# Ten token tiles of an output projection as 64-row products, and a dense stage whose order waits are PE's own

## The chip, the cores and the metric

The kernel runs on one core of one Trainium2 chip. The metric is the device time of one execution in microseconds: 1581.37 us for the kernel before, the median of 3 runs from 1580.71 to 1581.43.

PE is the engine of matrix products, with PEld its weight loads; ACT and DVE are the two engines that read the products' banks (PSUM), POOL a third vector engine without them, and SP issues most DMAs. Each engine takes its own instructions in the order in which the program lists them and waits on semaphores for the others.

## The reference, cut to what matters

```python
x = A_x                                   # 2048 tokens x 512
xn = layernorm(x)
qkv = xn @ wqkv                           # 32 heads of 16
p = softmax(q @ k.T * 16 ** -0.5)         # per head, 2048 x 2048
s = (p @ v) @ wo                          # 512 x 512
g = silu(gelu(xn @ w1 + b1) @ w2 + b2)    # hidden 1376
out = x + s * g
```

All inputs and the output are float32.

## The kernel before

*Number format.* A float32 product is made of three products of a reduced float32 form: each operand is split into a high and a low part, and `mm3` (L77) multiplies high by high, high by low and low by high into one bank. Scores take the three parts as 48 rows of one product instead; the products of probabilities and values (L804) are plain float32.

*Halves of PE.* A product with at most 64 contraction rows uses half of the array's rows. The kernel places such products in two kinds by rows: row half `a` = 0 stands on partitions 0 to 63, `a` = 1 on 64 to 127, and two products in different halves can run side by side. [...]

*Dense stage* (up to about 475 us). Layernorm and transposes come first. Then `run` (L614) issues lists of 64-row products for both halves in turn: the value projection (`quad`, L702), the query, key and hidden projections (`half`, L692) and the second matrix of the feed-forward part (`down`, L645). Between them `fill` (L563) places score products of the first heads' maxima (`s_one`, L203, whose product stands at L183), which DVE reduces (L189). All dense products go through `mm` (L583). It keeps for each bank (`key`) which half wrote it last and as which product. When a bank changes halves and that product isn't known to have ended (`prog["seen"]`, raised by `taken`, L577, since an older score product must have been reduced before a newer one takes its bank), `mm` needs a token: `mark` (L600) puts a copy of one element on ACT (L604) or DVE (L602), which waits for the newest product, and the next product of the new half waits for that copy. `down` sets marks ahead of need (`mark_early`, L608, at its fourth pair; two marks on DVE in its last but one part), `quad` one at its seventh pair.

*Attention stage.* It has 512 steps, `n`, in the loop at L966: 32 units `u` (4 heads and 512 queries each) by 16 blocks of 128 keys. A step's order on PE is written out as a string (`ORDER`, L40). T is a transposed score tile of 128 keys by 512 queries (`t_one`, L732, product L739), whose exponential ACT writes to SBUF (L741). S, X and Y are score products for maxima of later units (L183). V is the four value products of the step before (`pv_step`, L798), on the full rows in four column groups. Up to step 491 a step is `TSXTTSTYV`; from 492 on, when no maxima are left, `TTTTV`. The first two T of a step stand on half 1, the other two on half 0. T takes four banks in turn; a T waits until ACT has read its bank.

*Output stage inside the loop.* `todo` holds further work by step and place: what `at(n, f, ..., pos)` registers is issued after the T with that number (0 to 3) of step `n`. The output projection has 16 token tiles of 128. The first ten (`NW`) are placed from step `DONE` = 492 on, one each two steps:

- `load_gx` (L852), four steps before: two DMAs on SP bring the gate's input and x into `gx`, which has four buffers
- `w_token` (L881), two steps before: ACT copies the tile's four 128 x 128 blocks of the attention output to the high part (L876), POOL subtracts for the low part (L877)
- `w_mul` (L892): `mm3` for two of the four blocks at the tile's first step and for two at the second, after the step's last T, as products of all 128 rows; they add to one bank of a ring of three (`s_tile`, L92)
- `gate` (L863), at the first step: a tanh on ACT (L865) and a multiplication on DVE (L866)
- `w_out` (L913), at the second step: `w_gate` on DVE (L905) reads the bank, `w_add` on POOL (L910) adds x, and SP stores (L911)

Gates and loads of the last six tiles are placed at odd steps in between; their products come after the loop (L985 on), with moves and division of the last unit's output (`o_move`, `o_den`, `o_div`).

## Time and profile before

| What | Value |
|---|---|
| median of 3 runs | 1581.37 us |
| the profiled execution, its own time | 1580.84 us |
| its span | 1579.0 us |
| granted PE clock, mean of the core | 1.00 |
| PE busy | 1572.2 us in 12144 products |
| DVE busy | 1396.2 us in 2292 instructions |
| ACT busy | 1247.6 us in 2489 instructions |
| POOL busy | 373.6 us in 394 instructions |
| full-row products at L80 in the late stage | 10 tiles of 12, from 1492.7 us |

An instruction row of the timeline gives start, duration, engine, source line, operation, what it writes and reads, and in brackets the idle time of the engine before it with what ended it. Equal instructions in a row are joined (x2 and so on): the duration is then from the first start to the last end. A product's end is modelled, so starts tell more than durations. Rows of products name the output's tile: `pst` and `ps` are banks of different pools, `pv` that of the value products.

### The profile page before, as it was taken

What the parts mean: (1) busy time and instruction counts of PE and PEld (TensorE: products, weight loads), DVE (VectorE), ACT (ScalarE), POOL (GpSimd) and SP (SyncE); (2) the same over time, 40 slices, a digit from 0 to 9 for tenths busy, and PEclk for the clock granted to TensorE, in tenths of its full rate; (3) what the DMA queues carried; (4) which work ended last, traced back from release to release, by engine and by line L of the source; (5) the groups of instructions that cost most, each with busy time, mean ns of one, the idle gap of its engine ahead of it and who ended that gap; (6) DMA issues with size and microseconds to landing.
All of it is one profiled execution on the core that took longest, in us unless ns stands there. A gap on an engine that the chain in (4) does not pass through costs nothing.

```text
span 1579.0 us, 31736 instructions
## 1 busy us (share of the span) xinstructions
PE 1572.2 (100%) x12144; PEld 949.2 (60%) x12144; DVE 1396.2 (88%) x2292; ACT 1247.6 (79%) x2489; POOL 373.6 (24%) x394
## 2 busy tenths in 40 slices
PE   9999999999999999999999999999999999999998
PEld 8899899999994444444444444444444444444445
DVE  7599898989988999999999999999999999999734
ACT  4333443434339999999999999999999999999984
POOL 4145575766641001001000100100100000000143
PEclk9999999999999999999999999999999999999999
DMA  6626343454322114111511511421150111110252
GB/s 207 151 59 154 116 138 99 147 150 122 123 84 76 43 33 68 29 36 42 82 30 29 69 38 34 56 45 29 30 76 24 33 29 36 36 30 22 60 194 101
DMA packets 74647, 116.86 MB, mean 74 GB/s; under 512 B 23012, under 2 KB 24292, under 8 KB 73320
## 3 DMA queue, kind: packets, MB, share of 16 engines
q1 hardware_dynamic: 70748, 101.89, 24.1%
q0 software_dynamic: 3264, 12.35, 4.7%
q8 instruction: 96, 1.57, 0.5%
q10 hardware_dynamic: 484, 0.60, 0.1%
q14 instruction: 55, 0.45, 0.1%
HBM read 84.35 MB, written 25.97 MB: 70 GB/s over the span
## 4 chain that ended last, share of the span: by engine, by line
PE 98%; DVE 1%; DMA 0%; issue 0%; ACT 0%; DVEq 0%
PE pv L804 33%; PE pst L739 21%; PE ps L590 13%; PE ps L183 10%; PE pst L590 7%; PE ps L739 7%; PE ps L80 3%; PE pv L590 2%; PE ps L458 1%; PE pst L80 1%; DVE st L417 0%; PE pst L440 0%; DMA xt<-in_x 0%; PE pst L458 0%; DVE slot L75 0%; DVE xn L431 0%
## 5 line engine op out<-in xcount | busy, mean ns | idle before, releaser
L189 DVE TENSOR_REDUCE mx<-ps 128x2 f32<-128x512 f32 x2048 | 1298.3, 685 | 118.6 <-PE ps L183 33.0
L741 ACT ACTIVATE slot<-pst 128x512 f32<-128x512 f32 x1533 | 825.9, 603 | 19.9 <-PE pst L739 10.5
L804 PE MATMUL pv<-slot,vsb 128*32 128x512 f32 x4096 | 545.3, 605 | 0.0
L183 PE MATMUL ps<-kt,slot 48*128 48x512 f32 x1364 | 376.4, 366 | 0.0
L739 PE MATMUL pst<-qt,kt 50*128 50x512 f32 x1149 | 372.3, 431 | 0.6 <-DVE gt L672 0.4
L739 PEld LDWEIGHTS pst<-qt,kt 50*128 50x128 f32 x1149 | 188.6, 184 | 288.3 <-ACT slot L741 261.8
L741 ACT ACTIVATE slot<-ps 128x512 f32<-128x512 f32 x515 | 311.2, 605 | 2.7 <-PE ps L183 1.8
L183 PEld LDWEIGHTS ps<-kt,slot 48*128 48x128 f32 x1364 | 224.7, 184 | 8.2 <-DVE mx L189 5.9
L590 PE MATMUL ps<-slot,w1h 64*128 64x512 f32 x1088 | 218.0, 393 | 0.0
L183 PE MATMUL ps<-kt,qz 48*128 48x512 f32 x512 | 212.8, 416 | 0.0
L183 PE MATMUL ps<-slot,slot 48*128 48x512 f32 x598 | 165.5, 366 | 0.0
L739 PE MATMUL ps<-qt,kt 50*128 50x512 f32 x387 | 159.7, 415 | 0.0
L590 PEld LDWEIGHTS ps<-slot,w1h 64*128 64x128 f32 x1088 | 151.2, 185 | 8.2 <-ACT junk L604 2.4
L590 PE MATMUL ps<-slot,w1l 64*128 64x512 f32 x544 | 141.8, 393 | 0.0
L804 PEld LDWEIGHTS pv<-slot,vsb 128*32 128x32 f32 x4096 | 80.6, 108 | 100.0 <-issue 91.8
L377 POOL TENSOR_TENSOR hl<-hg,hh 128x512 fp32r<-128x512 f32 x76 | 96.7, 1295 | 129.6 <-ACT hh L376 97.5
L250 POOL CAST nmh<-nm 128x16 fp32r<-128x16 f32 x32 | 6.3, 196 | 480.4 <-DVE nm L247 458.0
L604 ACT ACTIVATE junk<-ident_r 1x1 f32<-1x1 f32 x92 | 18.0, 196 | 119.3 <-PE pst L590 116.1
L739 PE MATMUL pst<-qt,slot 50*128 50x512 f32 x384 | 111.2, 414 | 0.0
L183 PEld LDWEIGHTS ps<-kt,qz 48*128 48x128 f32 x512 | 93.7, 183 | 15.6
L183 PEld LDWEIGHTS ps<-slot,slot 48*128 48x128 f32 x598 | 98.3, 184 | 3.1 <-DVE mx L189 2.1
L739 PEld LDWEIGHTS ps<-qt,kt 50*128 50x128 f32 x387 | 71.1, 184 | 42.1 <-ACT slot L741 36.4
(159 smaller groups left out, 1707.2 us busy)
## 6 DMA issues: line engine op xcount, KB each, us to landing
raw<-in_w SPq DMA_DIRECT2D x88, 256.0 KB
qk_h<-hh SPq DMA_DIRECT2D x32, 256.0 KB
qk_l<-hl SPq DMA_DIRECT2D x32, 256.0 KB
qt<-qk_h SPq DMA_DIRECT2D x128, 64.0 KB
slot<-qk_h SPq DMA_DIRECT2D x92, 64.0 KB
g_d<-gt POOLq DMA_DIRECT2D x16, 256.0 KB, 3.8
qt<-qk_l SPq DMA_DIRECT2D x64, 64.0 KB
dn<-den_d SPq DMA_DIRECT2D x32, 128.0 KB
```

Source lines behind the costliest of these rows:

```text
L80: nc.tensor.matmul(ps, lhs[a], rhs[b], start=first and n == 0, stop=last and n == 2)
L183: return nc.tensor.matmul(ps[:, c0:c0 + w], QS[u][r, p, qi * P:(qi + 1) * P], kts[u // NCH % KB][p][r, k0:k0 + w], start=True, stop=True).ins
L189: nc.vector.tensor_reduce(MX[u][:, 2 * p:2 * p + 2, qi, ki][:, heads, parts], ps.rearrange("p (n c) -> p n c", c=HC), axis=AX.X, op=OP.max)
L250: nc.gpsimd.tensor_copy(hl[:, 0], nm)
L377: nc.gpsimd.tensor_sub(hl, raw, hh.bitcast(F32))
L458: nc.tensor.matmul(pq["q", g, c], W1[g][i][:, k * P:(k + 1) * P], (xh, xl)[j][c][:, k], start=n == 0 and k == 0, stop=n == 2 and k == KT - 1)
L590: i = nc.tensor.matmul(ps, lhs[r], rhs[r], start=first, stop=last).ins
L604: i = nc.scalar.activation(junk[:, :1], ident_r[:1, :1].bitcast(F32), AF.Copy).ins
L739: nc.tensor.matmul(ps, kts[g % KB][p][r, k * P:(k + 1) * P], QT[u][r, p, :], start=True, stop=True)
L741: nc.scalar.activation(PT[u, k][:, 2 * p + a, :], ps, AF.Exp, scale=SCALE)
L804: nc.tensor.matmul(PV[u][32 * j:32 * j + 32, :], vsb[:, k, h:h + 32], PT[u, k][:, j, :], start=(k == 0), stop=(k == NT - 1))
```

## The change

Three things change.

1. The first ten token tiles are taken in pairs. `w_two` splits two blocks of both tiles at a time. `w_halves` makes the products of one block of both tiles with 64 rows each: tile `t` on one row half and tile `t + 1` on the other, and at the next step the halves are exchanged. A pair takes four steps; six half products come after the step's second T (`pos=1`) and six after its last. The first product of a step after the pair's first waits for the last one of the step before (`HALF`).
2. Loads and gates are placed by pair: the load three steps before the pair's first step and two before (tile `t + 1`), gates at the first and the second step, both tiles' `w_out` at the fourth.
3. `mark`, `mark_early` and the copies of one element are gone. `mm` waits on PE's own semaphore for the product that wrote the bank last.

```diff
@@ mm
-        token = None
         if not first and writer[key][0] != a and writer[key][1] > prog["seen"]:
-            if not tokens or tokens[-1][0] < writer[key][1]:
-                mark()
-            prog["seen"], token = next(x for x in tokens if x[0] >= writer[key][1])
+            hold = nc.tensor.nop().ins
+            tc.add_manual_dep(hold, writer[key][2], SYNC, reason="other row tile")
+            prog["seen"] = writer[key][1]
         i = nc.tensor.matmul(ps, lhs[r], rhs[r], start=first, stop=last).ins
-        if token is not None:
-            tc.add_manual_dep(i, token, SYNC, reason="other row tile")
...
-        writer[key] = (a, prog["pe"])
+        writer[key] = (a, prog["pe"], i.name)
...
@@ down
-        n = prog["pe"]
-        if (c, f, part) == parts[-2]:
-            run(ops, {2: [lambda: mark(True)], 5: [lambda: mark(True)]})
-        else:
-            run(ops, {3: [lambda: mark_early(n)]})
+        run(ops)
@@ quad
-            hooks = {6: [mark]} if i in (1, 2) else {}
+            hooks = {}
@@ output stage
+    def w_two(t, k0):
+        oh, ol = [wb.tile([P, KT, P], F32R, name=x, bufs=3) for x in ("oh", "ol")]
+        c, i = divmod(t, NCH)
+        src = ot[c][:, k0:k0 + 2, i * P:(i + 2) * P]
+        hi, lo = [w.rearrange("p (k t) s -> p k (t s)", t=2) for w in (oh, ol)]
+        nc.scalar.activation(hi, src, AF.Copy)
+        nc.gpsimd.tensor_sub(lo, src, hi.bitcast(F32))
+        for k in range(2):
+            for j in range(2):
+                OTS[t + j, k0 + k] = (oh[:, 2 * k + j], ol[:, 2 * k + j])
+
+    HALF = {}
+
+    def w_halves(t, k, side):
+        ts = (t, t + 1)
+        if k == 0 and side == 0:
+            for i in ts:
+                PW[i] = [s_tile()[0]]
+        elif k % 2 == 0:
+            hold = nc.tensor.nop().ins
+            tc.add_manual_dep(hold, HALF[0].name, SYNC, reason="row tile done")
+        for n, (x, y) in enumerate(((0, 0), (0, 1), (1, 0))):
+            for a in range(2):
+                i = ts[a ^ side]
+                r = slice(64 * a, 64 * a + 64)
+                HALF[0] = nc.tensor.matmul(PW[i][0], OTS[i, k][x][r], (wo_h, wo_l)[y][r, k],
+                                           start=k == 0 and side == 0 and n == 0,
+                                           stop=k == KT - 1 and side == 1 and n == 2).ins
@@ placement
     for t in range(NW):
-        n = DONE + 2 * t
-        at(n - 4, load_gx, t)
-        at(n - 2, w_token, t)
-        at(n, w_mul, t, KS[:2])
-        at(n, gate, t)
-        at(n + 1, w_mul, t, KS[2:])
-        at(n + 1, w_out, t, nc.gpsimd)
+        n = DONE + 4 * (t // 2)
+        at(n - 3 + t % 2, load_gx, t)
+        if t % 2 == 0:
+            for i in range(4):
+                if i % 2 == 0:
+                    at(n + i - 2, w_two, t, i)
+                for j in range(2):
+                    at(n + i, w_halves, t, i // 2 * 2 + j, i % 2, pos=1 + 2 * j)
+        at(n + t % 2, gate, t)
+        at(n + 3, w_out, t, nc.gpsimd)
```

In the built program 92 copies on ACT, two on DVE and the waits for them are gone; the holds become waits of the next product on PE's own semaphore. PE has 120 products more (120 of full rows become 240 of half rows). ACT and POOL have as many splits as before, and SP as many DMAs.

More of the change, by code (lines that the diff above doesn't have):

```diff
@@ L584, in mm @@
         r = slice(64 * a, 64 * a + 64)
-        token = None
         if not first and writer[key][0] != a and writer[key][1] > prog["seen"]:
-            if not tokens or tokens[-1][0] < writer[key][1]:
-                mark()
-            prog["seen"], token = next(x for x in tokens if x[0] >= writer[key][1])
+            hold = nc.tensor.nop().ins
+            tc.add_manual_dep(hold, writer[key][2], SYNC, reason="other row tile")
+            prog["seen"] = writer[key][1]
         i = nc.tensor.matmul(ps, lhs[r], rhs[r], start=first, stop=last).ins
-        if token is not None:
-            tc.add_manual_dep(i, token, SYNC, reason="other row tile")
         prog["pe"] += 1
         row[a] += 1
-        latest[0] = (prog["pe"], i.name)
-        writer[key] = (a, prog["pe"])
-    tokens, latest = [], [None]
-    def mark(dve=False):
-        if dve:
-            i = nc.vector.tensor_copy(junk[:, 1:], ident_r[:1, :1].bitcast(F32)).ins
-        else:
-            i = nc.scalar.activation(junk[:, :1], ident_r[:1, :1].bitcast(F32), AF.Copy).ins
-        tc.add_manual_dep(i, latest[0][1], SYNC, reason="row tile done")
-        tokens.append((latest[0][0], i.name))
-    def mark_early(n):
-        if prog["seen"] < n:
-            mark()
-    junk = keep_r.tile([1, 2], F32, name="junk")
+        writer[key] = (a, prog["pe"], i.name)
     def run(ops, hooks={}):
@@ L657, in down @@
                                    f == 0 and part == 0 and n == 0, f == FT - 1 and part == 1 and n == 2))
-        n = prog["pe"]
-        if (c, f, part) == parts[-2]:
-            run(ops, {2: [lambda: mark(True)], 5: [lambda: mark(True)]})
-        else:
-            run(ops, {3: [lambda: mark_early(n)]})
+        run(ops)
         if part == 0:
```

## The prediction

> **What bounds the kernel now.** I read the first page, then the busy time by stretch, the chain in order of time, and the timeline of single steps.

> ```profile
> span 1579.0 us, 31736 instructions
> PE 98%; DVE 1%; DMA 0%; issue 0%; ACT 0%; DVEq 0%
> ```

> The profiled run took 1580.84 us: its span and 1.8 us around it, 0.53 under the median 1581.37. The chain is nearly all PE, but a busy PE is a modelled one, so the spacing of starts has to be read instead, stage by stage.

> ```profile
> 600.00:800.00 200.00, 200.00 (x1556) 93.97 (x1555) 188.11 (x312) 197.57 (x389) 24.47 (x37) 1.00 0.26 50
> 1497.50:1556.00 58.50, 58.50 (x326) 27.13 (x324) 20.77 (x26) 49.56 (x98) 27.96 (x20) 1.00 0.48 163
> ```

> Columns: span, then busy PE, PEld, DVE, ACT, POOL, clock, DMA share, GB/s. In the long attention stage, of which the first row is a part, ACT is busy 197.57 of 200, and no edit touches it. In the late stage, where the edited products stand, DVE has little left and ACT is busy 49.56 of 58.50.

> ```profile
> 1497.75 0.99 PE pv L804 x8
> ...
> 1556.20 1.85 PE pv L804 x16
> ```

> These rows of the chain are the value products of steps 494 and 512. 18 steps lie between: 58.45 / 18 = 3.247 us a step, ACT 49.56 / 18 = 2.75 of it. So PE's order sets the late step. One of them:

> ```profile
> 1505.19 0.73 PE L739 MATMUL pst<-qt,kt 50*128 50x512 f32 x3
> 1505.53 0.39 PE L739 MATMUL ps<-qt,kt 50*128 50x512 f32 x1
> 1505.85 0.50 PE L80 MATMUL ps<-wo_h,oh 128*128 128x512 f32 x1
> 1506.18 0.39 PE L80 MATMUL ps<-wo_l,oh 128*128 128x512 f32 x1
> 1506.41 0.39 PE L80 MATMUL ps<-wo_h,ol 128*128 128x512 f32 x1
> ...
> 1507.11 0.39 PE L80 MATMUL ps<-wo_h,ol 128*128 128x512 f32 x1
> 1507.42 1.06 PE L804 MATMUL pv<-slot,vsb 128*32 128x512 f32 x8
> 1508.42 0.51 PE L739 MATMUL pst<-qt,kt 50*128 50x512 f32 x2
> ```

> Four transposed tiles T0 to T3 (L739), six full-array output products (L80), four value products (L804). From the first T to V: 2.23 us; V to the next T: 1.00. A full-array product costs 0.23 (1506.18 to 1506.41). Around them is the loss: 0.32 from the last T to the first product (1505.53 to 1505.85) and 0.33 from that to the second, 0.65 for what two turns of 0.23 would be: 0.19 goes at the change from half arrays to the full array.

> **The change, part by part.**

> *Output products as halves.* Per token 12 products of 128 rows become 24 of 64 rows; two of them, on the two row halves, take the place of one. By step: T0, T1 on the upper half (both stand on rows 64 up), six half products, T2, T3 on the lower half, six half products, V. Each half gets 2 T and 6 products, eight turns, and nothing changes between half and full array before V. What a turn costs is seen in the dense stage, whose products are 64-row pairs already:

> ```profile
> 195.50 0.54 PE L590 MATMUL pst<-w2h,hl 64*128 64x512 f32 x2
> 195.65 0.20 ACT L604 ACTIVATE junk<-ident_r 1x1 f32<-1x1 f32 x1 [1.12 <-PE pst L590]
> 195.91 0.50 PE L590 MATMUL ps<-slot,w1h 64*128 64x512 f32 x1
> 196.25 0.40 PE L590 MATMUL ps<-slot,w1h 64*128 64x512 f32 x2
> 196.48 0.40 PE L183 MATMUL ps<-kt,qz 48*128 48x512 f32 x1
> 196.72 0.39 PE L590 MATMUL ps<-slot,w1l 64*128 64x512 f32 x2
> 196.95 0.63 PE L590 MATMUL ps<-slot,w1h 64*128 64x512 f32 x4
> ```

> Pairs start 0.233 apart (196.25 to 196.95 is three turns), and the first after an empty array takes 0.34 (195.91 to 196.25). The turn from the last product to V is taken as today, 0.31 (1507.11 to 1507.42). So T to V becomes 0.34 + 6 x 0.233 + 0.31 = 2.05 for eight turns, against 2.23: 0.18 a step. That needs the two halves to run as queues of their own, for in the program's order T1 stands before any work of the lower half. The trace shows it: T0, T1 come first and share their rows, yet

> ```profile
> 1505.19 0.50 PE L739 MATMUL pst<-qt,kt 50*128 50x512 f32 x2
> ```

> (a window cut short) has two T starting at once, and the fourth T, the one row named ps, starts 0.34 later, at 1505.53. Taken strictly in order it would be the third turn, 0.57 later. So T2 passed T1. The new order asks for no more: one product waiting on each half. Bounds: 1.94, if the weight load behind the first pair's 0.34 were hidden too, and 2.28, nine turns in strict order (0.34 + 7 x 0.233 + 0.31). I take 2.05, as the row speaks for the pass. [...]

> Nineteen steps give 19 x 0.18 = 3.4 us. The first late step is of another kind:

> ```profile
> 1491.18 1.04 PE L739 MATMUL pst<-qt,kt 50*128 50x512 f32 x3
> 1492.22 0.50 PE L739 MATMUL ps<-qt,kt 50*128 50x512 f32 x1
> 1492.65 0.50 PE L80 MATMUL ps<-wo_h,oh 128*128 128x512 f32 x1
> ...
> 1494.26 1.07 PE L804 MATMUL pv<-slot,vsb 128*32 128x512 f32 x8
> ```

> Here the T wait for ACT to empty their banks, T3 until 1492.22, and all six products wait behind it: 3.08 us to V. In the new order T3's turn comes at 0.34 + 3 x 0.233 = 1.04, just when its bank is free, with products before it. Saved 3.08 - 2.05 = 1.03; between 0.2 (ACT's wait is only moved) and 1.0 I take 1.0.

> *Tail.* POOL now adds token 8 and token 9 after the last step, in front of the split of token 11.

> ```profile
> 1556.13 1.92 PE L804 MATMUL pv<-slot,vsb 128*32 128x512 f32 x16
> 1556.24 0.69 DVE L905 SCALAR_TENSOR_TENSOR gx<-ps,gx 128x512 f32<-128x512 f32 x1 [1.70 <-PE ps L80]
> 1557.01 1.28 POOL L910 TENSOR_TENSOR gx<-gx 128x512 f32<-128x512 f32 x1 [1.33 <-DVE gx L905]
> 1558.24 1.28 POOL L877 TENSOR_TENSOR ol<-ot,oh 128x512 fp32r<-128x512 f32 x1
> 1558.99 1.16 SPq L827 DMA_DIRECT2D ot<-os  x2
> 1561.34 0.39 PE L80 MATMUL pst<-wo_h,ol 128*128 128x512 f32 x1
> 1561.41 0.33 SPq L833 DMA_DIRECT2D den_d<-dr  x1
> ```

> The split (L877) ended at 1559.52; with one more 1.28 it ends at 1560.8, and PE first needs it at 1561.34. SP's moves of the last unit (1558.99) stand behind a store that waits for the second addition; they start about 1.0 later and end at 1561.1, before the store of 1561.41. Between 0 and 0.5 late; I take 0.2.

> *Waits added in the late steps.* In 15 of the 20 steps the first half product waits on PE's own semaphore, for the last product of the step before, seven or eight matmuls back, with the whole V between: nothing. Behind it on PE stands the rest of the step. The split of the tokens into high and low parts (one ACT copy and one POOL subtraction for four 128 x 128 blocks, as many as before) is made two steps ahead, as before: nothing. Two tokens now end together, so the second bank is free one gate (0.69) later; of the three banks only the pair at step 496 takes both of the pair just ended, and its second product comes 0.57 after T0, 1.57 after V's start, against two gates (L905) that end 0.11 + 2 x 0.69 = 1.49 after it: nothing, or 0.2 once.

> *Gates early, loads.* ACT keeps its count, 2.75 a step within 3.07. The row loads stand three steps before their gate in SP's queue, behind two output stores instead of one.

> ```profile
> SPq L911 <- POOL gx L910: 34.9, 9, 6.1
> ```

> SP already stands 34.9 us in the late stage waiting for POOL before a store, and the loads behind it are in time. A second addition on POOL (1.28) makes them that much later, out of a lead of three steps of 3.05, 9 us. Were that cover gone, the gate's tanh would hold the exponentials behind it on ACT by the same amount. I take nothing.

> *Dense waits.* 92 small ACT operations and two on DVE go, each of which let PE wait for ACT to have seen a matmul end. In the new program 12 waits on PE's own semaphore remain, for matmuls at least 11 back (1.3 us at half a turn, 0.117, each), long ended.

> ```profile
> L604 ACT ACTIVATE junk<-ident_r x92: 182/202/205, 56.5 to 473.3; 1x1 f32<-1x1 f32 x92
> ...
>   PEld ps L590: 2.4, 9
> ```

> PE waited for them nine times, 2.4 us of weight loading in all. The fence of the dense stage shows one: the second of the two products at 195.50 starts at 195.65 (0.54 less its own 0.39 later), PE's next at 195.91, 0.26 on where 0.117 is half a turn, and the turn after that is 0.34 instead of 0.23; so the halves lose about 0.2. Bounds are 0 and 2.4; of the nine I count five as large as this one, 1.0. The 92 operations of 0.2 on ACT are no gain by themselves: PE, not ACT, has no gap there.

> Sum: -3.4 - 1.0 - 1.0 + 0.2 = -5.2. From 1580.84 that is 1575.6; at the median, 1576.2.

> **The rivals.**

> *Strict order* (nine turns): 19 x 0.05 longer, the first step 0.8 shorter, dense and tail as above: 0.95 - 0.8 - 1.0 + 0.2 = -0.65, 1580.7. Against it stands the pair at 1505.19; for it, that row shows a pass of one product once a step, while here one is needed at six turns in a row. [...]

> *Cover gone on ACT or SP*: late loads or a backlog before the exponentials. It would show as T waiting for ACT in steps with two extra ACT operations. ACT has 3.07 - 2.75 = 0.32 a step; half of the late gain lost makes -5.2 + 2.2 = -3.0: 1578.4.

> *Slower: each change of hands between T and products empties the half.* If the halves go in order and the weight load of the next product shows at each such change (T1 to product, product to T2, T3 to product), three turns cost 0.34 instead of 0.233 on top of nine: 2.28 + 3 x 0.107 = 2.60 from T to V. That is 19 x 0.37 = 7.0 longer, the first step 0.5 shorter, dense and tail as above: +5.7, 1587.1. It decides from the point where T to V is over 2.23. For it: a wait on a semaphore stands at two of the three places. Against it: in the dense stage the rows at 196.25 to 196.95 change between score and dense products (L183, L590) at the plain 0.233.

> **How the numbers follow.** Forecast 0.60, cover gone 0.14, strict order 0.14, slower 0.12. What a measurement can tell from no change is about 0.2%, 3.2 us. The forecast's own range is 1574 to 1578; strict order and half of the cover-gone case lie within 0.2%, and so does a tenth of the forecast: faster 0.54 + 0.07, rounded to 0.62; slower 0.12 and a little for what I did not see, 0.14; same 0.24. The range goes down to 1573.5 (late steps at 1.95 and dense waits at their bound) and up to 1584.5, past the strict order and into a mild case of the slower one; it leaves out about 0.1 above and 0.05 below.

> **What would show it.** In the new profile: L904 half products in pairs 0.23 apart, T to V 2.05 and the step near 3.05 in the chain; two T no longer starting together but each beside a product. Step 492 near 2.1 to V. No gap of 0.26 to 0.34 at the five dense places. The split of token 11 ending before its first use. Wrong would be: T to V of 2.28 or more; rows of ACT waiting for a load or of T for ACT in the late stage; PE waiting for POOL or a gate; a change in the long attention stage.

## The result and the profile after

| | before | after |
|---|---|---|
| median of 9 runs each, us | 1581.37 (1580.65 to 1581.85) | 1576.81 (1576.40 to 1577.34) |
| profiled execution, its span, us | 1580.84, 1579.0 | 1576.64, 1574.9 |
| first T after the dense stage | 474.00 | 473.26 |
| start of the last value products | 1556.13 | 1551.65 |
| from there to the end | 22.88 | 23.21 |

The ratio of the times is 0.9973 (95% interval 0.9963 to 0.9982): 0.27% faster. The medians differ by 4.56 us, the two profiled executions by 4.20 and their spans by 4.1; the account below goes by the spans. The forecast was a median of 1576.2.

Stretches of the changed kernel, with the columns as before (span, busy PE, PEld, DVE, ACT, POOL, clock, DMA share, GB/s):

```profile
600.00:800.00 200.00, 200.00 (x1555) 94.28 (x1555) 188.06 (x312) 197.61 (x388) 24.48 (x37) 1.00 0.26 50
1493.60:1551.60 58.00, 57.76 (x453) 30.77 (x449) 22.11 (x27) 51.62 (x102) 26.95 (x20) 1.00 0.51 170
```

The attention stage is what it was, with ACT busy 197.61 of 200. The late stage needs less time for a step (3.07 us instead of 3.25), and ACT's busy time in it rose from 49.56 of 58.50 us to 51.62 of 58.00: ACT is still idle at times, and the step still follows PE's turns.

One normal late step of the changed kernel, PE's timeline (start, us, engine, line, operation, tiles):

```profile
1531.20 0.50 PE L715 MATMUL pst<-qt,kt 50*128 50x512 f32 x1
1531.20 0.49 PE L904 MATMUL ps<-wo_h,oh 64*128 64x512 f32 x1
1531.54 0.39 PE L715 MATMUL pst<-qt,kt 50*128 50x512 f32 x1
1531.54 0.39 PE L904 MATMUL ps<-wo_l,oh 64*128 64x512 f32 x1
1531.76 0.39 PE L904 MATMUL ps<-wo_h,oh 64*128 64x512 f32 x1
1531.77 0.39 PE L904 MATMUL ps<-wo_h,ol 64*128 64x512 f32 x1
1532.00 0.39 PE L904 MATMUL ps<-wo_l,oh 64*128 64x512 f32 x1
1532.01 0.40 PE L715 MATMUL pst<-qt,kt 50*128 50x512 f32 x1
1532.23 0.39 PE L904 MATMUL ps<-wo_h,ol 64*128 64x512 f32 x1
1532.24 0.39 PE L715 MATMUL ps<-qt,kt 50*128 50x512 f32 x1
1532.46 0.41 PE L904 MATMUL ps<-wo_h,oh 64*128 64x512 f32 x2
...
1533.27 1.06 PE L780 MATMUL pv<-slot,vsb 128*32 128x512 f32 x8
```

Read it in pairs: a turn is one product on each half, and there are eight, 0.34 after the first and about 0.23 after each other one. T0 (L715) runs beside the first lower product, T1 beside the second. In the program T1 stands ahead of both lower products; it starts 0.34 after the first of them. From T0 to V it is 1533.27 - 1531.20 = 2.07 us.

Where the 4.1 us of span came from, by the starts of V in both traces (steps numbered as in the loop; the two V that the prediction called steps 494 and 512 are those of 493 and 511, and its count of 18 steps between them stands):

| Part | before | after | change |
|---|---|---|---|
| to the first T | 474.00 | 473.26 | -0.74 |
| from there to V of step 491 | 1016.19 | 1016.26 | +0.07 |
| step 492, V to V | 4.07 | 3.16 | -0.91 |
| 17 normal late steps, each | 3.25 | 3.07 | -3.1 |
| steps 496 and 497 together | 6.49 | 6.68 | +0.19 |
| last V to the end | 22.88 | 23.21 | +0.33 |

The changes add up to -4.2 (4.1 by the spans; the rest is rounding). Steps 496 and 497 are the place where the late stage fell short: they should have lost 0.36, as two normal steps do.

### The profile page after: what moved, and what is told of

The parts are those of the page before. It is cut to its first block, busy times and chain, and to the rows that moved or that the text cites. A ratio compares the mean times of both kernels' runs of the same rounds, so it can differ in the third digit from the quotient of the medians.

```text
span 1574.9 us, 31849 instructions
## 1 busy us (share of the span) xinstructions
PE 1567.4 (100%) x12264; PEld 951.9 (60%) x12264; DVE 1396.5 (89%) x2290; ACT 1233.8 (78%) x2397; POOL 371.7 (24%) x394
## 4 chain that ended last, share of the span: by engine, by line
PE 98%; DVE 1%; ACT 0%; DMA 0%; issue 0%; DVEq 0%
PE pv L780 33%; PE pst L715 21%; PE ps L589 12%; PE ps L183 10%; PE pst L589 7%; PE ps L715 7%; PE pv L589 2%; PE ps L904 1%; PE ps L80 1%; PE ps L458 1%; PE pst L80 1%; DVE st L417 0%; DMA xt<-in_x 0%; PE pst L440 0%; PE pst L458 0%
## 5 line engine op out<-in xcount | busy, mean ns | idle before, releaser
L715 PE MATMUL pst<-qt,kt 50*128 50x512 f32 x1149 | 380.1, 429 | 0.6 <-DVE gt L648 0.4
L183 PE MATMUL ps<-kt,slot 48*128 48x512 f32 x1364 | 376.0, 366 | 0.0
L715 PEld LDWEIGHTS pst<-qt,kt 50*128 50x128 f32 x1149 | 192.1, 184 | 288.1 <-ACT slot L717 272.3
L183 PEld LDWEIGHTS ps<-kt,slot 48*128 48x128 f32 x1364 | 224.9, 184 | 8.2 <-DVE mx L189 5.9
L183 PE MATMUL ps<-kt,qz 48*128 48x512 f32 x512 | 213.9, 418 | 0.0
L183 PE MATMUL ps<-slot,slot 48*128 48x512 f32 x598 | 165.3, 366 | 0.0
L715 PE MATMUL ps<-qt,kt 50*128 50x512 f32 x387 | 159.3, 414 | 0.0
L589 PEld LDWEIGHTS ps<-slot,w1h 64*128 64x128 f32 x1088 | 154.5, 185 | 4.5
L370 ACT ACTIVATE hg<-ps,b_sb 128x512 f32<-128x512 f32 x44 | 27.8, 684 | 132.0 <-PE ps L589 120.5
L715 PE MATMUL pst<-qt,slot 50*128 50x512 f32 x384 | 111.3, 414 | 0.0
L183 PEld LDWEIGHTS ps<-kt,qz 48*128 48x128 f32 x512 | 93.7, 183 | 19.4
L183 PEld LDWEIGHTS ps<-slot,slot 48*128 48x128 f32 x598 | 98.4, 184 | 3.3 <-DVE mx L189 2.1
L715 PEld LDWEIGHTS ps<-qt,kt 50*128 50x128 f32 x387 | 71.1, 184 | 42.3 <-ACT slot L717 36.1
```

The costliest lines, as they stand in the source:

```text
L183: return nc.tensor.matmul(ps[:, c0:c0 + w], QS[u][r, p, qi * P:(qi + 1) * P], kts[u // NCH % KB][p][r, k0:k0 + w], start=True, stop=True).ins
L370: nc.scalar.activation(raw, ph.pop(u), AF.Gelu_apprx_tanh, bias=b1_sb[:, u[2]:u[2] + 1])
L589: i = nc.tensor.matmul(ps, lhs[r], rhs[r], start=first, stop=last).ins
L715: nc.tensor.matmul(ps, kts[g % KB][p][r, k * P:(k + 1) * P], QT[u][r, p, :], start=True, stop=True)
```

## The experiments

All start from the changed kernel, except one that edits the kernel before; all but the mended kernel are single edits. Each ran once, except the mended kernel and the changed kernel beside it, so most readings are of one profile; a normal step's T to V differs by at most 0.03 us within a profile. Steps are read from V to V, "T to V" from the first T.

*By halves: how deep a row half's queue is at least.*

```diff
-        for n, (x, y) in enumerate(((0, 0), (0, 1), (1, 0))):
-            for a in range(2):
+        for a in range(2):
+            for n, (x, y) in enumerate(((0, 0), (0, 1), (1, 0))):
                 i = ts[a ^ side]
```

> Only the order inside a group of six half products changes: three on the lower row half, then three on the upper, where the changed kernel alternates. The theory (each row half is a queue of its own in which one product can wait, and PE takes its instructions in program order until the next finds that place full): counted turn by turn, nine turns from the first T to V instead of eight, 2.30 us where the changed kernel has 2.07; 19 steps, +4.4 us, a span near 1579.3. Rival, strict order (no product starts before one that stands ahead of it): twelve turns, 3.00 us, +18 us. Rival, two or more may wait on each half: eight turns, 2.07 us, no change.

The span is 1575.0 us, and T to V in the normal steps 2.07: no change. The theory's count was wrong, and the rival of two or more waiting products right; strict order would have cost 18 us by the count recorded above. (Step 497 is longer here than in the changed kernel; the last experiment takes that up.) The next run measures the depth.

*Deep: six products of one half ahead of anything for the other.* The order inside a late step becomes T0, T1 and six products on the upper half, then T2, T3 and six on the lower.

```diff
+        a = 1 - k % 2
...
-        for n, (x, y) in enumerate(((0, 0), (0, 1), (1, 0))):
-            for a in range(2):
-                i = ts[a ^ side]
+        i = ts[a ^ side]
+        for kk in (k - k % 2, k - k % 2 + 1):
+            for n, (x, y) in enumerate(((0, 0), (0, 1), (1, 0))):
```

> How many products can wait on one row half. In each late step the program's order is T0, T1 and six half products, all on the upper half, then T2, T3 and six half products on the lower. Counted turn by turn, the lower half stands idle until PE has put the upper half's products aside: with two places to wait a step has 13 turns, 3.21 us from T to V; with three 2.98; four 2.75; five 2.51; six 2.28; seven or more eight turns, 2.07 as in the changed kernel. Theory (the queues are no deeper than the two that the order by halves needs): 3.21 us, +1.14 a step, a span near 1597. Rival (deep queues): 2.07 to 2.3, a span of 1575 to 1580.

One step of this kernel, PE's timeline:

```profile
1531.17 0.72 PE L715 MATMUL pst<-qt,kt 50*128 50x512 f32 x2
1531.73 0.40 PE L906 MATMUL ps<-wo_h,oh 64*128 64x512 f32 x1
1531.97 0.39 PE L906 MATMUL ps<-wo_l,oh 64*128 64x512 f32 x1
1532.21 0.39 PE L906 MATMUL ps<-wo_h,ol 64*128 64x512 f32 x1
1532.21 0.50 PE L715 MATMUL pst<-qt,kt 50*128 50x512 f32 x1
...
1534.28 1.06 PE L780 MATMUL pv<-slot,vsb 128*32 128x512 f32 x8
```

Eight products of the upper half stand ahead of T2 in the program. T2 (the row of L715 at 1532.21) starts together with the fifth of them, ahead of the other three. That is the case of three places: 2.98 us was expected, and 0.107 more for T2's turn of 0.34 on a half that stood idle (T3 starts at 1532.55) makes 3.09; measured 3.11, a span of 1594.0. Depth two, the theory, is out by this row: T2 would have started with the sixth. That there are places, and three of them, is the author's count from these rows; the run doesn't tell whether they belong to each half or are shared by both: counted with three shared places, the order by halves has eight turns as well.

*After T: form or place.* All products behind the fourth T.

```diff
-                    at(n + i, w_halves, t, i // 2 * 2 + j, i % 2, pos=1 + 2 * j)
+                    at(n + i, w_halves, t, i // 2 * 2 + j, i % 2, pos=3)
```

> All twelve half products of a step stand behind the fourth T; none stand between the T. The theory (the gain of a normal late step comes from the form of the products, halves instead of the full array, and not from where they stand): eight turns again, T to V 2.05 to 2.10 us in the normal steps. The first late step, whose fourth T waits for its bank at 1.04 us with all products behind it, becomes 2.75 us instead of 2.17, so the span is some 0.6 us over 1574.9. Rival (the place between the T makes the gain): T to V stays at 2.23 or more in every step, a span of 1578 or more.

T to V in the normal steps is 2.06: the place earns nothing there, the form does. Step 492 of this kernel on PE's timeline:

```profile
1490.79 1.06 PE L715 MATMUL pst<-qt,kt 50*128 50x512 f32 x3
1491.84 0.50 PE L715 MATMUL ps<-qt,kt 50*128 50x512 f32 x1
1491.85 0.72 PE L904 MATMUL ps<-wo_h,oh 64*128 64x512 f32 x2
...
1493.67 1.07 PE L780 MATMUL pv<-slot,vsb 128*32 128x512 f32 x8
```

T3 waits until 1491.84 for its bank, and no product starts before it: 2.88 us to V against 2.17 with the products in between (2.75 was expected). So the place is worth 0.71 us, once. The span is 1575.9.

*Full products in between: the price of changing between half rows and the full array.*

```diff
-        for n, (x, y) in enumerate(((0, 0), (0, 1), (1, 0))):
-            for a in range(2):
-                i = ts[a ^ side]
...
+        i = ts[side]
+        mm3(PW[i][0], OTS[i, k], (wo_h[:, k], wo_l[:, k]), k == 0, k == KT - 1)
```

> The products keep their places between the T, but each pair of half products is one full-array product, three per group. The theory (each change between half rows and the full array costs): T0 to T1 0.34, to the first product 0.32, 0.33 and 0.23 within the three, 0.31 to T2, and the same again to V: 3.06 us from T to V instead of 2.07, steps of 4.06, 20 x 1.0 = 20 us more, a span near 1595. Without a cost of the change (ten turns of 0.233, the first 0.34, 0.31 to V) it would be 2.51 us and +9. Rival (the place alone earns): 2.07, no change.

PE's timeline of this kernel, the first half of a step:

```profile
1531.83 0.73 PE L715 MATMUL pst<-qt,kt 50*128 50x512 f32 x2
1532.49 0.50 PE L80 MATMUL ps<-wo_h,oh 128*128 128x512 f32 x1
1532.83 0.39 PE L80 MATMUL ps<-wo_l,oh 128*128 128x512 f32 x1
1533.06 0.39 PE L80 MATMUL ps<-wo_h,ol 128*128 128x512 f32 x1
1533.38 0.50 PE L715 MATMUL pst<-qt,kt 50*128 50x512 f32 x1
```

Each change shows twice, 0.32 before the first product of the new kind (1533.06 to 1533.38) and 0.34 after it (1532.49 to 1532.83), where a turn within a kind is 0.23. T to V is 3.10 (3.06 expected), the span 1594.8 (1595 expected). In this place the same multiplications as full products cost 20 us more than as halves.

*Near wait: when a wait on PE's own semaphore costs.*

```diff
-        elif k % 2 == 0:
+        else:
             hold = nc.tensor.nop().ins
             tc.add_manual_dep(hold, HALF[0].name, SYNC, reason="row tile done")
```

> A wait on PE's own semaphore is added in each of the 20 late steps, ahead of the second group of half products, for the last product of the first group, three products back with two T between (the waits of the changed kernel are for products seven or eight back). The theory (an own wait is free only where the awaited product has long ended): the second group starts when that product has ended, about 0.4 us after its start, which is some 0.2 us later than its turn, and its first turn is 0.34 instead of 0.23: T to V 2.37 us instead of 2.07, 20 x 0.3 = +6 us, a span near 1581. Rival (such a wait costs nothing at any distance): 2.07 and no change.

PE's timeline around one of the added waits:

```profile
1532.61 0.39 PE L904 MATMUL ps<-wo_h,ol 64*128 64x512 f32 x1
1532.61 0.40 PE L715 MATMUL ps<-qt,kt 50*128 50x512 f32 x1
1533.05 0.50 PE L904 MATMUL ps<-wo_h,oh 64*128 64x512 f32 x2
1533.39 0.39 PE L904 MATMUL ps<-wo_l,oh 64*128 64x512 f32 x2
```

The awaited product starts at 1532.61. The next pair starts 0.44 after it instead of 0.23, and the turn behind is 0.34: 0.31 us per wait. T to V is 2.38 (2.37 expected), the span 1581.2 (1581 expected). So a wait on PE's own semaphore three products back takes more than a step's whole gain of 0.18, while the 15 of the changed kernel, seven or eight back and with the whole V between, cost nothing: its normal steps have 2.06 to 2.08 with and without such a wait.

*The dense stage: three runs.* Marks back (the changed kernel with the old `mm`, `mark`, `down` and `quad`), dense only (the kernel before with the new ones), and the operations kept but awaited by nobody:

```diff
             if not tokens or tokens[-1][0] < writer[key][1]:
                 mark()
-            prog["seen"], token = next(x for x in tokens if x[0] >= writer[key][1])
+            hold = nc.tensor.nop().ins
+            tc.add_manual_dep(hold, writer[key][2], SYNC, reason="other row tile")
+            prog["seen"] = writer[key][1]
```

> The changed kernel with the dense waits of before: the 92 small ACT operations and the two on DVE are back. The theory (the dense stage's gain comes from the waits behind these operations): the first T after the dense stage starts near 474.0 us as before, 0.7 later than the changed kernel's 473.26, with the gaps on PE of 0.26 to 0.34 us back at five places; the late steps keep 2.07 from T to V; span near 1575.6. Rival (those 0.7 us are scatter between profiles): first T near 473.3.

> The kernel before with only the dense waits changed; the output products are whole, as before. The theory: first T near 473.3 us, 0.7 earlier than before's 474.0; the late steps stay at 3.25 us and T to V at 2.23; tail as before (22.9 us from the last value products to the end); span near 1578.3. Rival (the dense edit earns nothing): first T at 474.0, span 1579.0.

> The changed kernel with small ACT and DVE operations as before in the dense stage, but with nobody waiting for them: PE waits on its own semaphore as in the changed kernel. The theory (the gain is PE's wait, not ACT's 92 x 0.2 us): first T at 473.3 us as in the changed kernel, no gaps of 0.26 to 0.34 at the five places. Rival (ACT's time was the cost): first T near 474.0.

First T at 474.11, 473.29 and 473.23 us, spans 1575.4, 1578.4 and 1575.1. Dense only keeps T to V at 2.25 and the tail at 22.88. The same moment in two of the three, first with marks back, PE and ACT:

```profile
195.90 0.20 ACT L604 ACTIVATE junk<-ident_r 1x1 f32<-1x1 f32 x1 [1.11 <-PE pst L590]
196.16 0.18 PEld L590 LDWEIGHTS ps<-slot,w1h 64*128 64x128 f32 x1 [0.30 <-ACT junk L604]
```

and with the operations kept:

```profile
195.64 0.55 PE L591 MATMUL pst<-w2h,hl 64*128 64x512 f32 x2
195.79 0.20 ACT L603 ACTIVATE junk<-ident_r 1x1 f32<-1x1 f32 x1 [1.09 <-PE pst L591]
195.87 0.43 PE L183 MATMUL ps<-kt,qz 48*128 48x512 f32 x1
```

In the first, PE's weight load waits 0.30 for the small ACT operation; in the second the operation is still there (92 of them) and PE goes on. The starts of products near 161.4, 195.7, 229.9, 285.0 and 319.3 us have such gaps in the kernel before and with marks back, and in none of the runs without the waits that were compared (the changed kernel, by halves, dense only, operations kept). So the gain is PE's wait, and the ACT time was worth nothing that these runs can tell.

The moment of the first T scatters with the start of the program: it lay between 472.92 and 473.50 in eleven profiles without the waits and at 473.84 in a twelfth, that of the tail run below. Counted from one ACT row early in the dense stage (the first `hg` row after 100 us, 106.93 before and 107.03 after) it was 366.1 to 366.4 us in all twelve, 366.2 in the mean, and 367.1 and 366.9 in the two with the waits: some 0.8 us.

*Tail: what the last unit's denominators wait for.*

```diff
-        nc.sync.dma_start(out[t * P:(t + 1) * P, cs], gx[:, 0, cs])
+        n = 1 if t in (NW - 2, NW - 1) else P
+        nc.sync.dma_start(out[t * P:t * P + n, cs], gx[:n, 0, cs])
```

> The stores of tokens 8 and 9 carry one row of 128 each; the other 127 rows of these two tokens are not written. Everything else is the changed kernel. The theory for the tail (the last unit's denominators, dr<-os, land late since two row stores of 256 KB are on the DMA engines at the same time): the reciprocal starts 5.0 us after the last value products' start as before, instead of 5.74, PE has no gap ahead of the last chunk's products, and from the last value products to the end it is 22.9 us instead of 23.2. Rival (SP's queue, held by the store that waits for POOL's second addition, makes it late): SP still waits, so 23.2 stays.

The tail of the changed kernel (SP's and ACT's DMA issues, and DVE):

```profile
1553.85 1.59 SPq L916 DMA_DIRECT2D out<-gx  x2
...
1554.52 1.15 ACTq L800 DMA_DIRECT2D dr<-os  x1
1555.53 1.16 SPq L803 DMA_DIRECT2D ot<-os  x2
...
1557.39 0.25 DVE L808 RECIPROCAL dr<-dr 128x16 f32<-128x16 f32 x1 [2.91 <-DMA dr<-os]
```

and with one row in each of the two stores:

```profile
1555.13 1.14 ACTq L800 DMA_DIRECT2D dr<-os  x1
1556.04 1.16 SPq L803 DMA_DIRECT2D ot<-os  x2
...
1557.29 0.25 DVE L808 RECIPROCAL dr<-dr 128x16 f32<-128x16 f32 x1 [2.20 <-DMA dr<-os]
```

From the issue of `dr<-os` to the reciprocal it is 2.87 us in the first and 2.16 in the second (before: 2.14, from 1558.99 to 1561.13). SP's moves are late in both, 0.9 to 1.0 after that issue instead of beside it. So it is the stores' data that hold the denominators (2.87 us with 128 rows in each store, 2.16 with one), not SP's queue. From the last V to the end it is 22.94 us. Of the two, the landing is the firm reading: over all profiles the reciprocal started 5.6 to 5.8 us after the last V where a whole store was issued some 0.6 us behind `dr<-os`, as here, and 4.98 to 5.03 where none was: in the kernel before, in dense only, in this run, in the mended one below, and in the deep one and that with full products, whose two stores both go out ahead of it. The tail itself, from the last V to the end, is 22.87 to 22.96 us in the seven profiles without such a store (22.92 in the mean) and 22.94 (marks back) to 23.68 (near wait) in the seven with one (23.26 in the mean). Much of that scatter arises behind the reciprocal: from it to the last unit's division it took 5.60 us with marks back and 6.30 in near wait.

*Mended: the two long steps and the tail.*

```diff
         if k == 0 and side == 0:
+            if t == 2:
+                s_ring[:] = s_ring[2:] + s_ring[:2]
             for i in ts:
...
-        at(n + t % 2, gate, t)
-        at(n + 3, w_out, t, nc.gpsimd)
+        at(n + 1 + t % 2, gate, t)
+        at(n + 3, w_out if t < NW - 2 else w_gate, t, *[nc.gpsimd] * (t < NW - 2))
...
     o_move(NU - 1)
+    for t in (NW - 2, NW - 1):
+        nc.gpsimd.tensor_add(GX[t][:, 0], GX[t][:, 0], GX[t][:, 1])
...
     o_div(NU - 1, nc.vector)
+    for t in (NW - 2, NW - 1):
+        nc.sync.dma_start(out[t * P:(t + 1) * P, :], GX[t][:, 0])
```

> The changed kernel with three edits: the gates of a pair one step later, so that at step 496 the copy of the value sums does not stand behind a gate on DVE; the pair of step 496 takes another two of the three banks, so that neither waits for a gate of the pair just ended; the last pair's stores go out behind the last division. The theory (the two long late steps and the tail are these three): the steps of 2.29 and 2.39 us from T to V become 2.07, which is 0.55 us, the tail goes from 23.2 to 22.9, so the span is 0.85 us under 1574.9, some 1574.0, and the median near 1575.9, beyond which the comparison of medians can hardly tell. Rival (the stalls only move to the next step or to ACT): steps longer than 2.2 elsewhere and a span of 1574.9.

> The mended kernel again, on one chip with the changed one: the theory expects a median 0.85 us under the changed kernel's and a span near 1574.0. Rival (the gain is scatter between runs): medians within 0.3 us of each other.

> The changed kernel again, beside the mended one: a median near 1576.8 us, 0.85 over the mended kernel's; the same two long late steps of 2.29 and 2.39 us. Rival: within 0.3 us of the mended one.

The mended kernel holds three edits at once, so what each cures is read from the rows. The changed kernel at steps 496 and 497, the rows of all engines that matter:

```profile
1502.17 1.29 DVE L910 SCALAR_TENSOR_TENSOR gx<-ps,gx 128x512 f32<-128x512 f32 x2 [4.48 <-PE ps L904]
...
1503.05 0.49 PE L904 MATMUL ps<-wo_h,oh 64*128 64x512 f32 x1
...
1503.51 0.49 PE L904 MATMUL ps<-wo_l,oh 64*128 64x512 f32 x1
...
1505.52 0.64 ACT L884 ACTIVATE oh<-slot 128x512 fp32r<-128x512 f32 x1
1506.03 0.64 ACT L841 ACTIVATE slot<-gx 128x512 f32<-128x512 f32 x1
...
1506.23 1.30 POOL L885 TENSOR_TENSOR ol<-slot,oh 128x512 fp32r<-128x512 f32 x1 [0.71 <-ACT oh L884]
...
1506.70 1.37 DVE L842 SCALAR_TENSOR_TENSOR gx<-slot,gx 128x512 f32<-128x512 f32 x1 [3.25 <-ACT slot L841]
...
1508.00 0.68 DVE L787 COPY os<-pv 128x512 f32<-128x512 f32 x1
...
1508.73 0.64 PE L780 MATMUL pv<-slot,vsb 128*32 128x512 f32 x4 [0.24 <-DVE os L787]
```

the kernel before at step 496, ACT and DVE:

```profile
1507.65 0.65 ACT L865 ACTIVATE slot<-gx 128x512 f32<-128x512 f32 x1
...
1508.17 0.65 ACT L876 ACTIVATE oh<-slot 128x512 fp32r<-128x512 f32 x1
1508.33 0.69 DVE L866 SCALAR_TENSOR_TENSOR gx<-slot,gx 128x512 f32<-128x512 f32 x1 [3.34 <-DMA out<-gx]
```

and the mended one at the same place, DVE's timeline:

```profile
1502.15 1.29 DVE L912 SCALAR_TENSOR_TENSOR gx<-ps,gx 128x512 f32<-128x512 f32 x2 [1.41 <-PE ps L906]
1506.24 0.69 DVE L787 COPY os<-pv 128x512 f32<-128x512 f32 x1 [2.80 <-PE pv L780]
1509.24 0.69 DVE L842 SCALAR_TENSOR_TENSOR gx<-slot,gx 128x512 f32<-128x512 f32 x1 [2.31 <-ACT slot L841]
```

Two stalls are seen. At step 496 the second lower product (1503.51) follows the first by 0.46 instead of 0.34: the product ahead of it in the program, the first on the upper half, waits for its bank until the second gate (L910) ends at 1503.46, and PE's next products start only after that. T to V is 2.29. At step 497 V of the new unit needs the bank of the value sums, which DVE empties (L787); that copy stands behind the gate of token 2 (L842), and the gate took 1.37 us instead of 0.69. T to V is 2.39. The two are not independent: by halves and after T, whose step 496 has 2.06 to 2.08, step 497 has 2.62. The end of the copy stands where it stood, so the 0.55 us of both steps is the gate's, and the wait for the bank only takes a part of it earlier.

Why the gate took longer is in the rows too. The gate of token 2 stands at step 496 in both kernels, but ACT's order within the step has turned round: before, the tanh for the gate (1507.65) came ahead of the split's copy (1508.17), and the gate (1508.33) started before POOL's subtraction (1508.90); now the split's copy (1505.52) comes first, POOL starts its subtraction at 1506.23, and the gate starts behind it, at 1506.70. In the late steps of the changed kernel all eight gates that started while POOL was at a two-input operation took 1.31 to 1.41 us and ended 0.54 or 0.55 us after that operation; the other eight took 0.68 or 0.69. With 0.69 at step 496 the copy would have ended some 0.7 earlier, near 1508.0, ahead of V's turn (1506.34 + 2.07 = 1508.41); in by halves, where nothing waits for a bank, the same sum gives 1508.07 against 1508.25. So the longer gate alone accounts for the stall. A run with only the order of split and tanh turned back was not made.

In the mended kernel the copy starts at 1506.24 with V's end, both steps have 2.07 to 2.08, and the reciprocal of the tail starts 4.98 us after the last V.

On one chip the mended kernel ran in 1575.32 us (1575.25 to 1575.61, 5 runs; span 1573.5), the changed one in 1576.24 (1575.68 to 1576.47, 8 runs; span 1574.5), the one before in 1580.46 (1580.16 to 1581.22, 12 runs). That is 0.92 us between the first two where 0.85 was expected, and their runs do not overlap. On another chip the mended kernel ran in 1575.99 (1575.34 to 1576.28, 7 runs) against 1580.63 before. The ratios to before, 0.9967 (0.9955 to 0.9980) and 0.9970 (0.9958 to 0.9981), and for the changed kernel 0.9972 (0.9962 to 0.9983), overlap.

## Why the prediction was right, and by how much not

*Late steps: right.* 2.05 us from T to V was forecast and 2.07 came, 0.18 under the 2.25 that the late steps had before. Its ground, that a product on one row half may start ahead of an earlier one that waits for the other, holds: the strict order gives nine turns, 2.28 or more, and is seen in no normal step. The prediction asked for one waiting product; in the deep order T2 (1532.21) started ahead of three products that stand before it in the program. The two V that it called those of steps 494 and 512 are those of 493 and 511, which changes no sum.

*What earns: shown by removal.* With the products behind all T the normal step is the same, with full products between them it is 1.03 longer. So the form made the 3.1 us of the normal steps, by dropping the change between half rows and the full array. The 0.19 that the prediction read for that change is seen again where it is made oftener: 0.32 and 0.34 for two turns of 0.233.

*First late step: right in kind, 0.12 too large.* 1.03 was worked out and 1.0 taken; 0.91 came. Products behind all T put 0.71 of it back. Where the 0.12 stays was not followed.

*Gates early, loads, second bank: where it failed.* The prediction took nothing for the gates ("ACT keeps its count"), and for the second bank "nothing, or 0.2 once". The gate of token 2 cost 0.55 at steps 496 and 497 together. The prediction counted ACT's operations and SP's loads; it did not look at their order within a step, nor at DVE's queue, where the gate stands ahead of the copy that frees the value bank. The kernel before has the same order on DVE, with its gate at 0.69 us and no stall; the gate of 1.37 us ran while POOL subtracted (from 1506.23, for 1.30 us). It was one of eight such gates in the changed kernel, and all eight ended 0.54 or 0.55 us after the POOL operation that they met; what in the chip makes them longer no run shows. The wait for the second bank is real, 0.22 at step 496, and hidden in those 0.55. It is also one of the prediction's own signs of being wrong, PE waiting for a gate. The upper product's turn (1.57 after V's start) would have come after the gates' end (1.49 in the prediction, 1.41 in the trace), but the lower product behind it in the program came 0.12 late: the working left out that the products behind the waiting one in the program wait with it (the next lower one starts at 1503.51, the gates end at 1503.46).

*Dense waits: right, 0.2 to 0.3 too large.* -1.0 was forecast, -0.74 came by the first T and some -0.8 by the steadier count. The five places have their gaps with the waits and none without. Part of the gain is given back between the places: from marks back to operations kept, matched product by product, the lead grows by some 0.2 us at each place, and about 0.1 of it is lost again behind the first and the second. Why was not followed.

*Tail: size near, resource wrong.* +0.2 was forecast from POOL's additions and SP's late moves, +0.33 came; that the size is near is luck. SP's moves were late by the 1.0 that the prediction worked out and did not matter; the landing of the denominators did, 0.7 late beside the second store. One profile's tail can scatter by as much, but the means of the seven profiles with such a store and the seven without differ by 0.34 too.

*Rivals.* Strict order, cover gone on ACT or SP, and the emptying of a half at each change of hands were all priced at 1578.4 or more; none appeared as such. The stall on DVE is the nearest to "cover gone", on an engine that the prediction did not list.

The sum of -5.2 came out as -4.2: 0.55 at steps 496 and 497, 0.26 in the dense stage, 0.13 in the tail and 0.12 in step 492 make 1.06, the difference but for 0.06. About half of the shortfall is thus the stall on DVE. No errors cancelled: all four parts fell short.

One sum of the prediction does not come out: late steps at 1.95 (19 x 0.28 = 5.3) and 2.4 for the dense waits, with 1.0 and 0.2 for the first step and the tail, make -8.5, which is 1572.9 at the median and not the 1573.5 that the range names for it.

## What to carry to other kernels

Put products of 64 rows in one stream with others of 64 rows: in these rows a pair, one on each half, takes the same 0.23 us as one full product, and each change from half rows to the full array or back cost some 0.2 us (0.32 and 0.34 for two turns of 0.23). Put the products of a row half wherever their data are ready, as long as few of one half stand in a row: three against three in the order by halves kept T to V at 2.07 us, six in a row in the deep order made it 3.11. But keep waits for a semaphore away from the next few products: a wait on PE's own semaphore was free where the awaited product stood seven or eight back with V between (2.06 to 2.08 with and without it), and cost 0.31 us where it stood three back. All the kernels here wait before a bank changes halves; what comes without that wait no run shows. When work is moved, write down for every engine the order within a step before and after, and what stands behind each operation. Here a split moved ahead of a tanh, a gate on DVE started during POOL's subtraction and took 1.37 us instead of 0.69, and behind that gate stood the copy that frees a bank.
